# An attention and feed-forward kernel reordered by hand: woven stages, transposes by DMA, and a weight fold in fp16 halves

## Chip, cores, metric

The kernel runs on one core of a Trainium2 chip. The metric is device time in microseconds (us) of one execution. The core has five engines, each with its own queue of instructions, that meet by semaphores: TensorE (PE; its weight loads are the row PEld), VectorE (DVE), ScalarE (ACT), GpSimd (POOL) and SyncE (SP), which here only issues DMA transfers. Sixteen DMA engines carry all transfers.

Medians are over all runs of a kernel.

## The reference, cut to what matters

```
B = H = 8, S = 576 tokens, D = 64;  m = 32 landmarks, 18 tokens each
q_lm, k_lm = means of q, k over each landmark's 18 tokens
A  = softmax(q  @ k_lm.T / 8)     Bm = softmax(q_lm @ k_lm.T / 8)     C = softmax(q_lm @ k.T / 8)
Z  = Bm.T / (norm1(Bm) * norminf(Bm));   six times: Z = 2 Z - Z @ Bm @ Z
x  = A @ Z @ C @ v                        # 4608 x 512 over all batches and heads
out = ((x @ w1) * (x @ w2)) @ w3 @ w_out  # d_ff = 1024
```

Both kernels fold `w34 = w3 @ w_out` once, project `(Z C v)` through w1 and w2 per batch (`gt`), multiply by the normalised A (`up`: 64 products of 288 columns per batch), multiply the two results, and apply `w34` (`down`: 36 chunks of 128 tokens in all, 8 products of 512 columns each).

## The kernel before

The parts that the change touches. A tile scheduler may move instructions within what dependencies and buffers allow; the text order is not the issue order.

```python
CH = [(0, 128), (128, 128), (256, 128), (384, 128), (512, 64)]
    def load_attn(b):                       # 256-byte pieces: 64 floats of one head, one token
        ...
                nc.gpsimd.dma_start(out=qkn[0:sz, c, t, :]..., in_=src[b, :, s0:s0 + sz, :].rearrange("h p d -> p h d"))
    def attention(b, st):
        ...
                    nc.tensor.transpose(out=pst[:, 4 * t + r, 0:sz], in_=qkn[...], identity=ident16[...])
            ...                             # ScalarE or VectorE copies pst to qkT
                nc.vector.reduce_sum(out=lm[:, t, :, :], in_=qkT[:, t, :, :]..., axis=AX.X)
        ...                                 # qbd, B scores psB, C scores, A scores
        for it in range(6):                 # inverse chain on [residual | C v], 96 columns
            ...
                nc.vector.tensor_copy(out=nsz[:, :, 0:32], in_=pv_[:, :, 0:32])
                nc.vector.tensor_tensor(out=nsz[:, :, 32:96], in0=sz_[:, :, 32:96], in1=pv_[:, :, 32:96], op=ALU.add)
    def fold(pf):                           # fp32: TensorE transposes of w3, then products
        ...
    load(0); load_weights(); load(1)
    attention(0, sts[0]); fold(pf); attention(1, sts[1])
    for b in range(B):
        ...                                 # load(b + 2), attention(b + 1)
        project(sts[b]); up(sts[b], ab, S * (b % 2)); down(ab, t0, ...)
```

The softmax here doesn't subtract the row's maximum and nothing guards it: scores larger than these inputs give would overflow.

## Time and profile before

511.3 us (median; 510.3 to 512.5). The page's head, with the busy shares, and two rows of its picture of the span in 40 slices (tenths of busy time; tenths of full TensorE clock):

```profile
span 508.7 us, 8421 instructions
...
PE 356.7 (70%) x3584; PEld 210.3 (41%) x3584; DVE 215.1 (42%) x440; ACT 130.2 (26%) x213; POOL 80.7 (16%) x114
...
PE   0227179999765966696669476957695669476997
...
PEclk9999569999955896599659955995598669865999
```

No engine is full. The table by stretches (start:end and length; busy us and instructions for PE, PEld, DVE, ACT, POOL; granted clock; DMA share; GB/s) separates the stages:

```profile
core 0: us, PE busy (x) PEld busy (x) DVE busy (x) ACT busy (x) POOL busy (x), PEclk, DMA share, GB/s
0.00:62.00 62.00, 16.71 (x272) 10.36 (x272) 19.29 (x72) 6.69 (x11) 20.90 (x33) 0.89 1.33 200
69.00:135.00 66.00, 65.66 (x211) 33.58 (x209) 11.85 (x18) 5.45 (x9) 4.59 (x7) 0.97 0.37 63
184.00:234.00 50.00, 35.99 (x425) 21.89 (x423) 24.71 (x48) 15.72 (x26) 9.67 (x13) 0.76 0.56 71
```

Three readings. Until 62 us TensorE waits for batch 0's q and k, which come in small pieces. From 69 to 135 us the fold fills it. From 184 us every batch takes 50 us, of which TensorE is busy for 36 at a clock of 0.76. The longest chain of waits shows why: in each period one stage follows another, and a different engine holds each. These are some of its pieces in the period from 184 us (start, us, engine and line):

```profile
188.21 5.02 DVE lm L143 x2
193.25 0.43 DVE qbd L149
194.02 2.08 PE big L212 x20
...
202.60 0.90 PE small L260 x16
204.09 0.90 PE small L260 x16
...
209.95 1.06 DVE rr L297
...
217.03 8.53 PE big L342 x62
```

Line 143 is the landmark sum on VectorE, 149 the block-diagonal operand of the B scores, 212 the C scores, 260 the inverse chain (0.90 us of TensorE of every 1.49 us; most of the rest is VectorE), 297 a reciprocal, 342 the dense up products. The largest wait of TensorE from 184 to 485 us says the same (who waited for whom, us in total, times, longest):

```profile
PE small L160 <- DVE qbd L149: 37.1, 6, 6.2
```

So in every period TensorE stood 6.2 us for this operand; 5.0 us of it are the landmark sums.

### The profile page before, as it was taken

The numbers are of one execution on the slowest core, as the hardware profiler recorded it, in microseconds if no ns is written. First come the engines' busy times: TensorE is split into PE (matmuls) and PEld (weight loads), VectorE is DVE, ScalarE is ACT, GpSimd is POOL, SyncE is SP. The second block draws the span as 40 slices with busy tenths as digits, with TensorE's granted clock in tenths as the row PEclk, the third lists the DMA queues.
The fourth block names the chain that finished last, engine by engine and source line by source line (L and its number), as shares of the span: only waits on it lengthen the run. The fifth ranks groups of instructions, "written<-read, shape, count | busy, mean of one in ns | idle before, by whom it ended". The sixth has DMA issues, their size and how long they took to land.

```text
span 508.7 us, 8421 instructions
## 1 busy us (share of the span) xinstructions
PE 356.7 (70%) x3584; PEld 210.3 (41%) x3584; DVE 215.1 (42%) x440; ACT 130.2 (26%) x213; POOL 80.7 (16%) x114
## 2 busy tenths in 40 slices
PE   0227179999765966696669476957695669476997
PEld 0114054444343534363436253634353436253653
DVE  5034041111354635453545445544454454545450
ACT  0112000000220532153214321432153224322452
POOL 6231360000150025002400430034000000000000
PEclk9999569999955896599659955995598669865999
DMA  9999994120094039304920691049202000100012
GB/s 255 183 184 210 164 169 97 41 82 1 3 112 74 2 93 130 50 3 114 132 45 4 107 140 22 22 101 126 46 0 84 1 2 36 68 1 1 37 48 104
DMA packets 122037, 39.34 MB, mean 77 GB/s; under 512 B 113296, under 2 KB 113296, under 8 KB 122000
## 3 DMA queue, kind: packets, MB, share of 16 engines
q0 software_dynamic: 77120, 13.64, 33.6%
q1 hardware_dynamic: 42688, 18.88, 16.3%
q10 hardware_dynamic: 2192, 6.29, 3.4%
q8 instruction: 28, 0.46, 0.4%
q14 instruction: 9, 0.07, 0.0%
HBM read 42.99 MB, written 9.44 MB: 103 GB/s over the span
## 4 chain that ended last, share of the span: by engine, by line
PE 63%; DVE 17%; DMA 10%; ACT 5%; issue 2%; POOL 2%; ACTq 0%; POOLq 0%
PE big L342 13%; PE small L356 12%; PE small L380 11%; DVE lm L143 7%; PE small L260 6%; DMA qkn<-in_q_dram 6%; DMA qkn<-in_k_dram 5%; PE big L322 5%; PE small L227 4%; ACT qkT L137 3%; PE big L212 3%; PE small L277 2%; PE big L307 2%; DVE rr L297 2%; PE big L373 2%
## 5 line engine op out<-in xcount | busy, mean ns | idle before, releaser
L342 PE MATMUL big<-ahat,gt 128*128 128x288 f16 x512 | 71.7, 287 | 2.6 <-DVE gt L330 1.6
L106 POOL DMA_DIRECT2D qkn<-in_q_dram x40 | 35.4, 884 | 236.6 <-PE pst L132 215.3
L356 PE MATMUL small<-w_133,ab 128*128 128x512 f16 x288 | 63.5, 379 | 0.0
L342 PEld LDWEIGHTS <-gt 128*128 128x128 f16 x512 | 48.3, 97 | 28.8 <-issue 5.6
L348 DVE TENSOR_TENSOR ab<-a_sb,big 128x576 f16<-128x576 f16 x64 | 48.3, 755 | 23.1 <-ACT a_sb L347 19.6
L380 PE MATMUL small<-wof,w3t 128*128 128x512 f32 x128 | 56.7, 599 | 0.3 <-DVE w3t L377 0.3
L132 PE MATMUL pst<-ident_84,qkn 128*128 128x128 f16 (+1 forms) x320 | 24.6, 223 | 35.6 <-DMA qkn<-in_q_dram 20.8
L347 ACT CAST a_sb<-big 128x576 f16<-128x576 f32 x64 | 40.8, 638 | 31.5 <-PE big L342 31.5
L139 DVE COPY qkT<-pst 128x1024 f16<-128x1024 f16 x16 | 11.1, 692 | 81.9 <-PE pst L132 81.9
L143 DVE TENSOR_REDUCE lm<-qkT 128x128 f16<-128x2304 f16 x16 | 40.1, 2548 | 7.3 <-ACT qkT L137 7.3
L356 PEld LDWEIGHTS <-ab 128*128 128x128 f16 x288 | 28.2, 98 | 32.5
L106 POOL DMA_DIRECT2D qkn<-in_k_dram x40 | 35.2, 880 | 14.3 <-DMA wdup<-in_moe_w_dram 8.3
L132 PEld LDWEIGHTS <-qkn 128*128 128x128 f16 (+1 forms) x320 | 19.7, 100 | 42.1 <-DMA qkn<-in_q_dram 21.9
L160 PE MATMUL small<-lm,qbd 128*64 128x32 f16 x32 | 2.3, 225 | 49.4 <-DVE qbd L149 49.4
L380 PEld LDWEIGHTS small<-wof,w3t 128*128 128x128 f32 x128 | 24.1, 192 | 29.1 <-issue 28.3
L359 ACT ACTIVATE o_sb<-small 128x512 f32<-128x512 f32 x36 | 21.5, 597 | 44.7 <-PE small L356 44.7
L377 DVE COPY w3t<-big 128x512 f32<-128x512 f32 x16 | 10.7, 689 | 50.0 <-PE big L373 33.2
L283 ACT ACTIVATE zt<-small 128x256 f16<-128x256 f32 x8 | 3.1, 383 | 106.1 <-PE small L277 106.1
L137 ACT COPY qkT<-pst 128x1024 f16<-128x1024 f16 (+1 forms) x24 | 20.8, 868 | 30.0 <-PE pst L132 30.0
L322 PE MATMUL big<-wdup,zt 128*32 128x512 f16 x256 | 25.9, 575 | 0.3 <-ACT gt L328 0.3
L330 DVE TENSOR_SCALAR gt<-big 128x1024 f16<-128x1024 f32 x16 | 19.5, 1225 | 15.4 <-PE big L322 15.3
L328 ACT ACTIVATE gt<-big 128x1024 f16<-128x1024 f32 x16 | 16.3, 1023 | 35.3 <-PE big L322 35.3
(265 smaller groups left out, 344.4 us busy)
## 6 DMA issues: line engine op xcount, KB each, us to landing
out_dram<-o_sb SPq DMA_DIRECT2D x36, 256.0 KB, 2.0
vt<-in_v_dram SPq DMA_DIRECT2D x32, 256.0 KB, 4.9
w3f<-in_moe_w_dram ACTq DMA_DIRECT2D x8, 512.0 KB, 4.0
qkn<-in_q_dram POOLq DMA_DIRECT2D x32, 128.0 KB, 4.7
qkn<-in_k_dram POOLq DMA_DIRECT2D x32, 128.0 KB, 4.9
wdup<-in_moe_w_dram POOLq DMA_DIRECT2D x4, 1024.0 KB, 22.7
wof<-in_moe_w_out_dram ACTq DMA_DIRECT2D x1, 2048.0 KB, 10.8
vt<-in_v_dram SPq DMA_DIRECT2D x8, 128.0 KB, 5.0
```

The lines of the kernel that those rows point to most:

```text
L106: nc.gpsimd.dma_start(out=qkn[0:sz, c, t, :].rearrange("p (h d) -> p h d", d=D), in_=src[b, :, s0:s0 + sz, :].rearrange("h p d -> p h d"),)
L132: nc.tensor.transpose(out=pst[:, 4 * t + r, 0:sz], in_=qkn[0:sz, c, t, 128 * r:128 * r + 128], identity=ident16[0:sz, 0:sz])
L137: nc.scalar.copy(out=dst, in_=pst[:, :, 0:sz])
L143: nc.vector.reduce_sum(out=lm[:, t, :, :], in_=qkT[:, t, :, :].rearrange("p r (l g) -> p r l g", g=GRP), axis=AX.X,)
L260: nc.tensor.matmul(psI[sl, 96 * qd + (32 if last else 0):96 * qd + 96], sz_[sl, qd, 0:32], sz_[sl, qd, (32 if last else 0):96], start=True ...
L322: nc.tensor.matmul(psG[32 * h:32 * h + 32, n, :], st["zt"][:, 4 * qd + h, :], wdup[:, 4 * qd + h, w, 512 * n:512 * n + 512], start=True, s ...
L342: nc.tensor.matmul(p[:, c, 0:HS], st["g"][qd][:, w, 128 * j:128 * j + 128], st["ahat"][qd][:, c, :], start=(qd == 0), stop=(qd == 1))
L347: nc.scalar.copy(out=a_sb, in_=ps[0][:, :, 0:HS])
L348: nc.vector.tensor_tensor(out=ab[:, j, off:off + S].rearrange("p (c s) -> p c s", c=2), in0=a_sb, in1=ps[1][:, :, 0:HS], op=ALU.mult)
L356: nc.tensor.matmul(pso[:, :], ab[:, j, 128 * t:128 * t + 128], w34[:, j, :], start=(j == 0), stop=(j == 7))
L359: nc.scalar.activation(out=o_sb, in_=pso[:, :], func=AXF.Copy, scale=1.0 / (X64 * X64))
L380: nc.tensor.matmul(psW[:, :], w3t[:, c4, :], wof[:, c, :], start=(c == 0), stop=(c == 7))
```

## The change

Its intent: no scheduler, but an order written by hand, in which pieces of the attention of batch b+2 and of the inverse chain of b+1 lie between up and down products of batch b; fewer, longer load pieces; q, k and w3 transposed by DMA from on-chip memory to on-chip memory; the fold as four fp16 products of high and low halves instead of one in fp32; an inverse chain that carries only Bm-sized blocks. The diff, cut to its core (definitions of tiles and unchanged arithmetic are left out):

```diff
+    ctx.enter_context(tc.manual_schedule())
+    def load_qk(b, st):                       # 96 partitions, 6 tokens each: 1.5 KB per piece
+            nc.gpsimd.dma_start(out=n, in_=src[b].rearrange("h (p x) d -> p h (x d)", p=P))
+    def turn_qk(b, st):
+            nc.sync.dma_start_transpose(out=t.rearrange("p h j s -> p (h j) s"),
+                in_=st[name + "n"].rearrange("p h x -> p (h x)"))
-                    nc.tensor.transpose(out=pst[:, 4 * t + r, 0:sz], ...)
-            ... nc.scalar.copy / nc.vector.tensor_copy(out=dst, in_=pst[:, :, 0:sz])
+    def landmarks(b, st):
+        for name in ("k", "q"):
+            nc.vector.tensor_reduce(out=lp, in_=st[name + "T"]..., axis=AX.XY, op=ALU.add)
+            nc.vector.tensor_copy(out=lx[0:64], in_=lp[64:128])     # the two halves hold
+            nc.scalar.copy(out=lx[64:128], in_=lp[0:64])            # even and odd tokens
+        ... lmk = lp + lx;  qbd = lp + lx
...
-        for it in range(6):  # 96 columns, two VectorE operations per step
+    def istep(b, st, it):    # 64 columns, one VectorE operation
+            nc.vector.tensor_tensor(out=d4[:, :, 0:2, :], in0=s4[:, :, 0:3:2, :], in1=pv_, op=ALU.add)
...
+        def split_w3(j):
+            nc.scalar.activation(out=s[:, 0, :], in_=t, func=AXF.Copy, scale=WS)
+            nc.vector.scalar_tensor_tensor(out=s[:, 1, :], in0=t, scalar=WS, in1=s[:, 0, :], op0=ALU.mult, op1=ALU.subtract)
+            nc.sync.dma_start_transpose(out=w3t.rearrange("p a c j -> p (a c) j"), in_=s.rearrange("p a c -> p (a c)"))
+        def prod(j, c):
+            for a, bb in ((0, 0), (1, 0), (0, 1), (1, 1)):
+                nc.tensor.matmul(psw[j], w3ts[j][:, a, c, :], woh[:, c, bb, :], ...)
...
+    def spread(main, other):                  # lays `other` evenly between `main`
+    for f in fold[:16]:
+        f()
+    spread(fold[16:], front(0) + ... + back(0)[:7] + front(1) + back(0)[7:])
     for b in range(B):
+        main = []                             # 8 up units with the held down chunks of b-1 strewn in
+        ...
+            turn_qk(b + 2, sts[b + 2]); load_v(b + 2, sts[b + 2]); load_qk(b + 3, sts[b + 3])
+        ...                                   # other = front(b+2) mixed with the chain of b+1, then project(b+1)
+        spread(main, other)
+        held = [down chunks of b]
```

`front` begins with the landmarks and the B scores of its batch.

## The prediction

> **What bounds the kernel now.** The span is 508.7 us and no engine is full: the page gives TensorE 70%, VectorE 42%, ScalarE 26%. The chain of waits shows three stages. (1) Start: batch 0 waits for its q, k pieces until 62 us (113,296 of 122,037 packets are under 512 B). (2) The fp32 fold w3*w_out, 69 to 135 us: dense TensorE, 10.5 us per 24 products (437 ns each), plus transposes. (3) From 184 us, a serial period of 50.1 us per batch: 16 us of full up/down products (64 of 288 columns in 7.9 us, 32 or 40 of 512 in 6.9 or 8.65 us) and 34 us of attention and projection, where each engine waits for another: transposes and copies 4 us, landmark sums 5.0 us, 1.3 to 1.5 us per inverse step, reciprocals. There the table by stretches shows TensorE 60 to 75% busy at a granted clock of 0.5 to 0.75.
>
> **What the change does.** Emission order becomes execution order: attention of b+2 and the inverse chain of b+1 lie between up and down products of b, so latency should be paid in parallel. The TensorE transposes of q, k (24.6 us busy) and their copies (32 us on ScalarE, VectorE) go; two DMA transposes per batch replace them. Loads become 1.5 KB runs. Chain steps are 64 columns instead of 96, with one vector operation instead of two. The fold becomes 256 fp16 products (down shows 216 ns at 512 columns: 55 us against 66), which hide attention 0 and 1. Added: about 26 us of splitting on ScalarE and VectorE, GpSimd sums, a copy across partitions after the landmark sums.
>
> Transpose time is an estimate: the Trainium skill, "DMA: Bandwidth & Descriptors" (Latency and other measured facts), gives 261 GB/s for one transpose; 0.59 MB gives 2.3 us, plus its 2.0 us fixed cost: 4.3 us. No run here shows it yet.
>
> **A woven batch.** TensorE: up 7.9, down 7.8, scores 3, C*V 1.5, chain 3.5, Z, denominators, normalising 2.5, projection 2 to 3: 29 to 31 us. VectorE: up 6.0, landmarks 7.3, projection 2.4, rest 9: 25 us. TensorE bounds, but not alone: landmarks hold VectorE for 7 us in one piece, while TensorE has one down chunk and one up unit (3 us) ahead of the B scores that need them. I expect a 4 to 5 us hole per batch there: 37 us per period instead of 50 (six periods: minus 78).
>
> **Start.** Fold from about 18 to 20 us, thin until all weight pieces and first transposes are through (SyncE carries all transposes in one queue). Then 48 fold units (41 us) woven with 21 us of attention, plus stalls. First up product at about 118 us, against 169 now: minus 50. Last batch and final down: unchanged.
>
> Sum: 118 + 6x37 + 25 (batch 6: up, down, chain, projection) + 15 + 10 = 390; I shade to 383, since fuller activity should raise the granted clock.
>
> **Predicted: 383 us, 8 in 10 within 348 to 425. Faster by over 2%: 0.96; within 2%: 0.02; slower: 0.02.**
>
> **Right, if:** TensorE above 80% in the middle with clock above 0.9; period 35 to 39 us; largest TensorE wait the B scores on VectorE's landmarks; transposes landing in 4 to 6 us; fp16 fold at 216 ns each. **Wrong, if:** transposes land in over 10 us, so landmarks wait for DMA; VectorE over 85% busy; fold stretched by late weights, start beyond 130 us.
>
> **What would make it wrong.** Slow transposes (sixteen, and eight for the fold, in one queue) would push it beyond 420. If the in-order queues interlock less than I think, 345.

## The result and the profile after

The changed kernel takes 409.4 us (median of 5; fast runs 406.0 to 409.4), before 511.3 us. The ratio is 0.7975, interval 0.7943 to 0.8008. (A ratio is the mean time of one kernel's fast runs over that of the other's of the same rounds, so it is not quite the ratio of the medians.) Executions over 1.5% slower than the fastest of the same kernel are left out of the means. The measured time lies within the predicted range, 26 us above its centre. The profiled run is one of the slow ones (414.7 us), so its numbers are compared below with care.

The page's head and picture after:

```profile
span 413.0 us, 8352 instructions
...
PE 287.4 (70%) x3552; PEld 161.6 (39%) x3552; DVE 216.1 (52%) x437; ACT 128.0 (31%) x201; POOL 45.1 (11%) x72
...
PE   0007703999479847949949890898298639999995
...
PEclk9999965999959959979987996699699959999999
```

The stretches after, with the same columns:

```profile
0.00:33.70 33.70, 0.00 (x0) 0.00 (x0) 12.36 (x47) 7.51 (x7) 3.77 (x10) 1.00 1.07 228
33.70:47.70 14.00, 13.94 (x58) 6.01 (x59) 4.63 (x3) 2.60 (x3) 0.78 (x1) 1.00 1.12 257
47.70:68.30 20.60, 1.49 (x8) 0.50 (x7) 4.69 (x7) 1.40 (x3) 0.77 (x1) 0.65 1.26 158
68.30:141.00 72.70, 64.04 (x685) 29.64 (x685) 34.04 (x72) 16.73 (x25) 10.78 (x16) 0.89 0.88 147
141.00:399.00 258.00, 198.54 (x2764) 121.12 (x2761) 158.87 (x307) 96.12 (x158) 29.03 (x44) 0.89 0.45 93
```

TensorE does nothing until 33.7 us, and almost nothing again from 47.7 to 68.3 us. The loop from 141 us has TensorE busy 198.5 of 258 us, 77%, where before it was 72% of a longer period, at a clock of 0.89 instead of about 0.75. TensorE's waits over the whole run:

```profile
PE small L442 <- DMA w3t<-w3s: 60.4, 3, 33.8
PE small L157 <- DVE qbd L149: 46.7, 6, 11.7
PE small L386 <- DVE xd L239: 2.5, 2, 1.3
```

Line 442 is the fold: it waited for transposed w3 three times, 60.4 us in all. Line 157 is the B scores: six waits of 7.8 us in the mean and 11.7 at most, 46.7 us in all. Everything else is small. Between the first and the last up product the trace has six spells in which the granted clock is 0.5, and each begins within one of the six waits for the B scores. The longest wait lasts from 247.7 to 259.3 us, and the clock is 0.5 from 251.7 to 265.4 us. How long the transposes took, from issue to landing (median):

```profile
w3t<-w3s SPq DMA_TRANSPOSE x8, 12.4
kT<-nat SPq DMA_TRANSPOSE x8, 6.1
qT<-nat SPq DMA_TRANSPOSE x8, 5.4
```

The q and k transposes have medians of 6.1 and 5.4 us. Those of w3 have a median of 12.4 us, a minimum of 4.5 and a maximum of 24.9. SyncE's own queue at the start and around one landmark stage (start; us from the first instruction's start to the last one's end, gaps between them included; instructions):

```profile
8.78 24.67 SPq L432 DMA_TRANSPOSE w3t<-w3s  x2
...
34.18 8.33 SPq L78 DMA_TRANSPOSE kT<-nat  x1
...
47.70 44.93 SPq L432 DMA_TRANSPOSE w3t<-w3s  x4
```

```profile
210.25 34.62 SPq L397 DMA_DIRECT2D out_dram<-o_sb  x10
245.46 3.06 SPq L78 DMA_TRANSPOSE kT<-nat  x1
248.71 3.07 SPq L78 DMA_TRANSPOSE qT<-nat  x1
```

Of the two w3 transposes in the first line, one is issued at 8.8 us (it lands at 33.7) and the other at 21.4. In the second fence the q, k transposes are issued at 245.5 and 248.7 us, right after the ten output stores of the iteration before, the last of which waited for the last down chunk. VectorE's landmark sums then waited for both transposes (4.1 and 2.3 us), and TensorE for the sums, until 259.3 us.

### The profile page after: what moved, and what is told of

Its sections match the earlier page's. It is cut to its first block, busy times and chain, and to the rows that moved or that the text cites. A ratio compares the mean times of both kernels' runs of the same rounds, so it can differ in the third digit from the quotient of the medians.

```text
span 413.0 us, 8352 instructions
## 1 busy us (share of the span) xinstructions
PE 287.4 (70%) x3552; PEld 161.6 (39%) x3552; DVE 216.1 (52%) x437; ACT 128.0 (31%) x201; POOL 45.1 (11%) x72
## 4 chain that ended last, share of the span: by engine, by line
PE 57%; DMA 19%; DVE 14%; ACT 5%; issue 4%; SPq 0%; ACTq 0%; DVEq 0%
PE small L386 15%; DMA w3t<-w3s 14%; PE small L442 14%; PE big L373 13%; DVE lp L137 6%; DMA qT<-nat 5%; PE small L291 3%; PE big L210 3%; PE big L330 3%; PE small L232 3%; ACT a_sb L378 2%; DVE ab L379 2%; DVE gt L337 1%; PE big L248 1%; ACT gt L335 1%
## 5 line engine op out<-in xcount | busy, mean ns | idle before, releaser
L442 PE MATMUL small<-woh,w3t 128*128 128x512 f16 x256 | 67.8, 410 | 61.2 <-DMA w3t<-w3s 60.4
L373 PE MATMUL big<-ahat,gt 128*128 128x288 f16 x512 | 80.6, 304 | 0.9 <-DVE gt L337 0.5
L386 PE MATMUL small<-w,ab 128*128 128x512 f16 x288 | 69.6, 388 | 4.5 <-DVE xd L239 2.5
L442 PEld LDWEIGHTS <-w3t 128*128 128x128 f16 x256 | 24.1, 103 | 91.1 <-DMA w3t<-w3s 61.4
L373 PEld LDWEIGHTS <-gt 128*128 128x128 f16 x512 | 48.4, 103 | 22.7 <-issue 4.4
L157 PE MATMUL small<-lmk,qbd 64*32 64x32 f16 x64 | 1.9, 195 | 46.7 <-DVE qbd L149 46.7
L220 POOL TENSOR_TENSOR e<-ect 96x384 f32<-96x384 f32 x16 | 16.0, 999 | 164.5 <-ACT ect L215 82.6
L137 DVE TENSOR_REDUCE lp<-kT 128x256 f32<-128x2304 f16 x8 | 20.4, 2548 | 8.6 <-DMA kT<-nat 8.5
L137 DVE TENSOR_REDUCE lp<-qT 128x256 f32<-128x2304 f16 x8 | 20.4, 2553 | 7.5 <-DMA qT<-nat 7.4
L291 PE MATMUL small<-sz 32*32 32x64 f32 (+1 forms) x768 | 20.6, 224 | 1.5 <-DVE sz L298 1.5
L298 DVE TENSOR_TENSOR sz<-sz,small 128x128 f32<-128x128 f32 x40 | 11.4, 284 | 16.8 <-PE small L291 16.5
L429 DVE SCALAR_TENSOR_TENSOR w3s<-w3f,w3s 128x1024 f16<-128x1024 f32 x8 | 9.8, 1222 | 18.2 <-ACT w3s L428 18.2
```

Source lines behind the costliest of these rows:

```text
L137: nc.vector.tensor_reduce(out=lp, in_=st[name + "T"].rearrange("p h j (l g) -> p h l j g", g=3), axis=AX.XY, op=ALU.add)
L220: nc.gpsimd.tensor_tensor(out=e3, in0=ect[:, 0:3], in1=ect[:, 3:6], op=ALU.add)
L291: nc.tensor.matmul(psI[sl, 64 * qd:64 * qd + n], src[sl, qd, 32:64], src[sl, qd, 0:n], start=True, stop=True, tile_position=(32 * h, 32 * h))
L373: nc.tensor.matmul(p[:, c, 0:HS], st["g", qd][:, w, 128 * j:128 * j + 128], st["ahat", qd][:, c, :], start=(qd == 0), stop=(qd == 1))
L386: nc.tensor.matmul(pso[:, :], ab[:, j, 128 * t:128 * t + 128], w34[:, j, :], start=(j == 0), stop=(j == 7))
L442: nc.tensor.matmul(psw[j], w3ts[j][:, a, c, :], woh[:, c, bb, :], start=(c == 0 and a + bb == 0), stop=(c == 7 and a + bb == 2))
```

## The experiments

Twelve kernels ran. All gave correct results. Each was timed in three rounds beside the kernel before, which stayed at 509.7 to 511.4 us. To separate the start from the loop I read when the first and the last group of up products (line 373 or its counterpart) began.

| kernel | median us | ratio to before | first up, us | first to last up, us |
|---|---|---|---|---|
| changed kernel | 409.4 | 0.7975 | 141.0 | 258.5 |
| the same again | 410.8 | 0.7983 | 136.4 | 260.7 |
| early turn | 395.3 | 0.7737 | 134.5 | 242.3 |
| early turn and early sums | 400.2 | 0.7845 | 138.1 | 246.5 |
| w1, w2 load later | 418.4 | 0.8191 | 145.2 | 257.8 |
| w3 turned on TensorE | 403.0 | 0.7865 | 125.4 | 257.9 |
| no weave in the loop | 461.7 | 0.9026 | 166.5 | 276.0 |
| two operations per step | 414.1 | 0.8089 | 142.7 | 260.0 |
| chunks first | 404.9 | 0.7959 | 136.3 | 252.9 |
| copy off ScalarE | 412.3 | 0.8062 | 135.2 | 260.4 |
| chunks first, copy off ScalarE | 376.8 | 0.7353 | 136.2 | 222.2 |
| those, start mended | 357.4 | 0.6948 | 117.1 | 224.9 |
| those, fold in fp32 | 342.6 | 0.6700 | 102.3 | 231.7 |

(The "no weave" loop emits attention before its first up unit, so its two columns are not comparable with the others. The last two columns are of the profiled run alone. The profiles of the changed kernel, "the same again", "two operations" and "fold in fp32" fell in slow runs.) Kernels with the start of the changed kernel show the first up product at 134.5 to 138.1 us in fast profiles, and at 136.4 and 141.0 us in the two slow ones, so differences of a few us in that column mean nothing.

**The changed kernel again.** Unaltered, beside other variants.

> The changed kernel once more, unaltered, to have it on the same chip and in the same rounds as the variants beside it, and a profile in the fast state. Expected 405 to 410 us; first up product at 138 to 142 us, TensorE's wait for the B scores' operand 44 to 48 us.

As expected in its times (median 410.8 us; fast runs 406.2 and 409.3) and its waits (47.6 us for the B scores); the first up product, at 136.4 us, came a little before the stated range.

### What made the loop wait

**Early turn.** Theory A blames SyncE's queue order, theory B the VectorE work itself.

```diff
+        if b + 3 < B:
+            fr.insert(8, lambda n=b + 3: bring(n))   # turn_qk, load_v, next load_qk: mid iteration
-        if b + 2 < B: turn_qk(b + 2, ...) ...        # was: start of the next iteration
```

> Only the place of the q, k DMA transposes in SyncE's queue changes: those of batch b+3 are issued in the middle of iteration b instead of at the start of iteration b+1, so they no longer stand behind that iteration's last output stores. Theory A (queue order: the hole before the B scores is partly the late transposes): VectorE's waits for the kT and qT DMA (16 us in all) vanish from the middle, TensorE's wait of 46.7 us on qbd (six waits, mean 7.8, longest 11.7) falls to about 30 us (mean 5), and the time falls by 10 to 16 us. Theory B (the hole is VectorE's own 7 to 8 us of landmark work): the wait stays above 42 us and the time moves by under 5 us.

Measured 395.3 us. VectorE's waits for kT and qT fell from 15.9 us to 0.5, and TensorE's wait became:

```profile
PE small L157 <- DVE qbd L149: 32.7, 6, 7.0
```

Six waits of 5.5 us, four of them of 5.2. Theory A is confirmed for 14 us of waiting (12 to 13 us of time by the ratios). What remains is a wait for VectorE's landmark work, which itself hardly waits for a transpose any more; the prediction had put it at 4 to 5 us.

**Early turn and early sums.** The sums also move to the end of the iteration before, in three pieces.

```diff
+            other.insert(k3 - 7, lambda: lm_sum(n3, s3, "k"))
+            other.insert(k3 - 3, lambda: lm_sum(n3, s3, "q"))
+            other.append(lambda: lm_join(n3, s3))
+        if b > 0 and fr:
+            fr.pop(0)                                # landmarks no longer at the head of front
```

> As the early turn, and the landmark sums of batch b+3 are also made at the end of iteration b, in three pieces laid between other work, instead of in one piece in front of the B scores. Theory A+B (both late transposes and the 7 us piece): TensorE's wait on qbd falls under 8 us and the time falls by 25 to 40 us against the changed kernel. Rival (VectorE is nearly full, the sums only move the hole): the wait goes to other VectorE results (gt, ab, psum slots) and the time falls by under 15 us.

Measured 400.2 us, 5 us slower than the early turn. The wait for the B scores fell to 10.7 us, and new ones came:

```profile
PE big L336 <- ACT a_sb L384: 13.8, 6, 2.9
PE small L163 <- DVE qbd L150: 10.7, 5, 7.0
PE small L392 <- DVE xd L245: 7.7, 2, 3.9
```

The rival holds: the hole moved, here to the projection (line 336), which waits for PSUM that ScalarE has not yet emptied.

**Chunks first.** Instead of moving the sums, give TensorE work under them: the down chunks need no VectorE, only a copy by ScalarE.

```diff
+        main = ups
+        if fr:
+            other.pop(0)()          # landmarks(b + 2)
+        for f in held:              # then all 4 or 5 down chunks
+            f()
         spread(main, other)
```

> Only the order in an iteration changes: landmarks of b+2, then all held down chunks (4 or 5, 7 to 8.7 us of TensorE that need only ScalarE to drain), then up units woven with the rest. Theory: the hole before the B scores is TensorE running out of work that does not need VectorE; the chunks fill it and the output stores leave SyncE's queue early. Then TensorE's wait on qbd falls from 46.7 to under 10 us and the time falls by 25 to 35 us, to 372 to 384. Rival (as the early sums showed: VectorE's 25 us then collect behind the up units instead): the time falls by under 16 us, no better than the early turn alone.

Measured 404.9 us: five of the six waits for the B scores are gone (the one left, 5.7 us, is in the first iteration), and the time has hardly moved. TensorE's waits and ScalarE's queue in one landmark stage:

```profile
PE small L386 <- ACT o_sb L389: 22.7, 5, 4.5
...
PE small L157 <- DVE qbd L149: 5.7, 1, 5.7
```

```profile
206.88 0.40 ACT L142 COPY lx<-lp 64x256 f32<-64x256 f32 x1 [4.35 <-DVE lp L137]
209.79 0.40 ACT L142 COPY lx<-lp 64x256 f32<-64x256 f32 x1 [2.51 <-DVE lp L137]
210.22 1.08 ACT L389 ACTIVATE o_sb<-small 128x512 f32<-128x512 f32 x2
```

ScalarE's next instruction after the projection was `lx` (line 142), the copy of the landmark sums' other half. It waited 4.35 us and then 2.51 us for VectorE's sums. The chunks' output copies (line 389) were behind it, so two finished chunks kept both small PSUM buffers (TensorE's result memory) until ScalarE began to empty them at 210.2 us. TensorE stood meanwhile, 22.7 us in five such waits. The Trainium skill, "TensorE: Matmul & The Clock Gate" (the table at its head), calls the queues of ScalarE, VectorE and GpSimd "strict FIFO"; this trace agrees.

**Chunks first, and the copy off ScalarE.** One line more.

```diff
-            nc.scalar.copy(out=lx[64:128], in_=lp[0:64])
+            nc.vector.tensor_copy(out=lx[64:128], in_=lp[0:64])
```

> As the chunks first, with one line more: the copy of the landmark sums' lower half into the upper partitions is made by VectorE, not ScalarE. Theory: in the chunks-first run ScalarE stood in its queue at this copy, which waits for VectorE's 2.5 us sums, so the chunks' output copies behind it came late and TensorE ran out of PSUM (22.7 us on o_sb in five waits). Then those waits fall under 4 us and the time falls by 15 to 24 us against chunks first, to 381 to 390. Rival (TensorE's freed time is only given back behind VectorE, which gets 0.6 us more per batch): under 8 us.

Measured 376.8 us, 28 us less than with the order alone in the medians and 31 by the ratios, more than expected.

```profile
PE small L291 <- DVE sz L298: 9.6, 7, 1.5
PE small L157 <- DVE qbd L149: 7.6, 4, 6.3
```

The loop of chunks first, and of this kernel, with the columns of the stretches above:

```profile
136.00:389.00 253.00, 199.69 (x2770) 119.20 (x2763) 158.55 (x309) 95.67 (x158) 29.09 (x44) 0.94 0.48 96
136.20:358.40 222.20, 190.33 (x2767) 117.20 (x2764) 162.06 (x320) 91.48 (x147) 29.05 (x44) 0.98 0.55 110
```

The wait on `o_sb` is gone from the table, the one on qbd is 7.6 us, and the loop has shrunk to 222.2 us, with TensorE busy 190 us of it, 86%. The gain over chunks first is larger than the 22.7 us of waits because TensorE's busy time fell as well, by 9 us, at a granted clock of 0.98 instead of 0.94.

**The copy alone.** The fourth corner: the one-line edit just shown, made in the changed kernel without the new order.

> The changed kernel with only the copy of the landmark halves moved from ScalarE to VectorE, the order left as it is: the fourth corner beside the changed kernel (about 409), chunks first (405) and both (377). If the two only work together (in the given order TensorE stands at the B scores anyway, and what ScalarE holds back has nobody waiting): within 6 us of the changed kernel, wait on qbd still above 40 us. If the copy on ScalarE was the fault by itself: faster by 15 us or more.

Measured 412.3 us, wait on qbd 50.8 us. So of two edits that alone change next to nothing (ratios 0.7959 and 0.8062, against 0.7975 and 0.7983 of the changed kernel), both together are worth 32 us (0.7983 less 0.7353, times 510). In the order as given TensorE stood at the B scores in any case, and no large wait on ScalarE shows; with the order mended, the copy was the next thing in the way. (That the same copy spoiled the early sums, too, is likely, since line 336 waited for ScalarE, but no run took it away there.)

**No weave.** How much is the weaving worth at all?

```diff
-        spread(main, other)
+        for f in other: f()
+        for f in main: f()
```

> In each iteration of the loop all attention pieces of later batches are emitted first, then the held down chunks and up units; nothing else differs (the start is still woven, chain and attention of two batches are still mixed). If the gain of the loop comes from laying latency under up and down products: period 42 to 46 us instead of 36, time 440 to 465 us. Rival (the gain comes from the shorter work itself: no TensorE transposes, no copies, shorter chain, and weaving adds little since the engines block each other in order): time under 425 us.

Measured 461.7 us. The ratio says that the loop's weave gives about 53 us of the 103 us gained (0.9026 against 0.7983, times 510). The rest, by subtraction, is the start and the shorter work; no run separates these two. Without the weave TensorE's clock in the loop is back at 0.75, and its waits for the sums grow from 47.6 to 64.0 us, those for the chain (line 298) from 1.5 to 9.6. In the middle the first up products of two batches lie 44 to 48 us apart, a little above the stated 42 to 46.

**Two operations per step.** The chain's one VectorE operation becomes two again, still on 64 columns.

```diff
-            nc.vector.tensor_tensor(out=d4[:, :, 0:2, :], in0=s4[:, :, 0:3:2, :], in1=pv_, op=ALU.add)
+            for i in range(2):
+                nc.vector.tensor_tensor(out=d4[:, :, i, :], in0=s4[:, :, 2 * i, :], in1=pv_[:, :, i, :], op=ALU.add)
```

> Each inverse step's addition is cut into two VectorE operations, as the kernel before had it: 40 more operations of about 0.2 us, 8 us of VectorE in all. If the chain's latency is hidden under other work: the time rises by under 4 us. If the chain still bounds: it rises by 8 us or more.

Measured 414.1 us, between the two marks: the means of fast runs differ by 5.4 us. The loop in the profile, 260.0 us, is not longer than that of the same kernel again (260.7), and the difference lies before the first up product (142.7 against 136.4 us), where two runs of one kernel differed by 4.6. Both profiles are of slow runs. So the chain's latency appears to be hidden in the loop; the total is inconclusive.

### What made the start late

**The w1, w2 load later.**

```diff
-    load_weights()
     turn_qk(0, sts[0])
     load_qk(1, sts[1])
+    load_weights()
```

> The 4.2 MB load of w1, w2 is issued after batch 1's q, k loads instead of before them. Theory C (the first two weight transposes, issued at 8.8 us and landed at 33.7, are slow because they share the 16 DMA engines with 7 MB of loads): they land by about 20 us, fold starts there, and the time falls by 5 to 14 us, some given back where the load now meets the next transposes. Rival D (transposes are slow by themselves): first fold product stays at 30 us or later and the time does not fall.

The first fold product came at 21.8 us instead of 33.8, so the first transposes had been slowed by the loads beside them (theory C), and D falls. But the time rose by 9 us in the medians, 11 by the ratios. The first two lines are of the changed kernel, the others of this one:

```profile
33.76 15.42 PE L442 MATMUL small<-woh,w3t 128*128 128x512 f16 x64 [33.76 <-DMA w3t<-w3s]
68.29 5.30 PE L442 MATMUL small<-woh,w3t 128*128 128x512 f16 x12 [19.11 <-DMA w3t<-w3s]
...
21.76 16.38 PE L442 MATMUL small<-woh,w3t 128*128 128x512 f16 x64 [21.76 <-DMA w3t<-w3s]
61.77 5.30 PE L442 MATMUL small<-woh,w3t 128*128 128x512 f16 x12 [23.64 <-DMA w3t<-w3s]
...
82.72 1.89 PE L442 MATMUL small<-woh,w3t 128*128 128x512 f16 x4 [9.21 <-DMA w3t<-w3s]
```

The load now met the next transposes, and the fold's second wait became 23.6 us, with a third of 9.2. The collision was only moved. My expectation had the sign of the total wrong.

**w3 turned on TensorE.** The same halves, transposed through PSUM (16 transposes of 128x128 per block).

```diff
-            nc.sync.dma_start_transpose(out=w3t..., in_=s...)
+            for a in range(2):
+                for c in range(8):
+                    nc.tensor.transpose(out=pst[:, a, c, :], in_=s[:, a, 128 * c:128 * c + 128], identity=ident16[:, :])
+            nc.scalar.copy(out=w3t[:, 0], in_=pst[:, 0])
+            nc.vector.tensor_copy(out=w3t[:, 1], in_=pst[:, 1])
```

> The w3 halves are transposed on TensorE (16 of 128x128 per block, through PSUM, half copied by ScalarE and half by VectorE) instead of by DMA. If the 60.4 us that TensorE waited for w3t are the cost of the start, the fold starts at about 12 us, its middle gaps go, the first up product comes at 110 to 118 us instead of 141, and the time falls by 22 to 32 us. Rival: the fold is then held by the weight loads themselves (last w_out piece landed at 22 us) or by q, k of batch 0, and under 12 us come back.

Measured 403.0 us, about 6 us less. The first up product came at 125.4 us, 9 to 13 us earlier than in the fast profiles with the start as it was; the loop was unchanged. (This profile is of the kernel's fastest run, 398.5 us.) The rival was nearer: the fold's first products came at 27.8 us, not 12. TensorE turned the first half at 11.4 us, but the copies of the result stood in ScalarE's queue behind the splitting of later pieces, the last of which waited for its load of w_out until 25.7 us. TensorE's two longest waits (first line: B scores; second: turning of w3):

```profile
PE small L159 <- DVE qbd L151: 58.2, 8, 11.9
PE pst L441 <- ACT w3s L430: 19.1, 2, 11.4
```

**Start mended.** The mended loop, w3 turned on TensorE, w1, w2 loaded later (now harmless), and seven fold units in a row while the landmarks of batches 0 and 1 are made.

```diff
+    gap = [lambda: None] * 7
+    pro = (f0[:1] + gap + f0[1:] + ... + f1[:1] + gap + f1[1:] + back(0)[7:])
```

> The former, plus the start mended: w3 halves turned on TensorE, the w1, w2 load behind batch 1's q, k (now no weight transposes are left for it to meet), and seven fold units in a row while landmarks of batches 0 and 1 are made. First up product at 105 to 115 us against 136 to 141; time lower than the former by 22 to 35 us, 350 to 365. Rival (start bound by load bandwidth): first up product still after 122 us.

Measured 357.4 us; first up product at 117.1 us. 19 us less than the mended loop alone, a little under the expected 22 to 35 (21 by the ratios). The three changes of the start were made together, so their shares are not known.

**The fold in fp32.** As the kernel before computed it, in the mended kernel.

```diff
-        (split_wo, split_w3; four fp16 products per unit)
+            nc.tensor.transpose(out=pst[:, c, :], in_=s[:, 128 * c:128 * c + 128], identity=ident[:, :])   # fp32
+            nc.tensor.matmul(psw[j], w3ts[j][:, c, :], wof[:, c, :], start=(c == 0), stop=(c == 7))
```

> The former, with the fold as the kernel before computed it, in fp32 (64 products, which that trace shows as 128 records of 437 ns: 56 us against 55 for 256 fp16 products), so the splitting of w3 and w_out, 26 us of ScalarE and VectorE, goes, and only 64 transposes remain, of about 0.15 us. If the fp16 halves only repay what they cost: within 6 us of the former either way. If they were worth having: slower by over 8 us.

Measured 342.6 us, another 15 us less in the medians and 13 by the ratios, which none of the stated outcomes had. The first fold product comes at 17.9 us instead of 27.8, the last at 100.8 instead of 115.8:

```profile
L453 PE MATMUL small<-woh,w3t x256: 379/379/634, 27.8 to 115.8; 128*128 128x512 f16 x128
```

```profile
L435 PE MATMUL small<-wof,w3t x128: 592/592/1061, 17.9 to 100.8; 128*128 128x512 f32 x128
```

The span of products is about as long (83 against 88 us): in both kernels a whole block of w3 takes 7.0 to 7.1 us of TensorE where it runs dense. What goes is the splitting between load and transpose, and half of the transposes and copies. The order of the first loads changed as well (w3 before w_out), so the 10 us by which the fold begins earlier are not shown to be due to the splitting alone. Against the changed kernel this version is about 65 us faster by the ratios, and it beats both kernels.

## Why the prediction was right or wrong

- **Direction and range: right.** 409.4 us in 348 to 425. The sum of its terms was 390, shaded to 383.
- **The term that was mis-sized is the start.** "First up product at about 118 us" measured 141.0 and 136.4 us (134.5 to 138.1 in fast profiles of kernels with the same start). The step that failed in it is "Fold from about 18 to 20 us": it began at 33.8 us, and stood again until 68.3. The prediction had the single queue of transposes right, but took their time as 4.3 us each. For q and k in the loop, most of them 5.0 us and none over 8.3, that was nearly right; for w3, beside 160 to 260 GB/s of transfers up to 68 us, the median is 12.4 us and the worst 24.9. Its own test ("start beyond 130 us") caught this. The rest of the sum fits the profiled run: 141.0 us, six periods of 37.1 and 49.6 for the end make its span of 413 us, where the prediction had 118, 37 and 50.
- **"37 us per period": right in size, for partly other reasons.** From the first up product of batch 0 (141.0 us) to that of batch 6 (363.4 us) the six periods take 37.1 us each. TensorE's hole at the B scores was there, the largest wait of the loop as foreseen, but 7.8 us and not 4 to 5. Some 2.3 us of the hole are transposes behind output stores in SyncE's queue (early turn: 14 us over six waits). TensorE's own work was smaller than the 29 to 31 us of the sum: 27 us of busy time per period (163.4 us over the six). A hole taken 3 us too small and work taken 2 to 4 us too large offset each other, which is luck.
- **"TensorE above 80% in the middle with clock above 0.9": missed,** 77% and 0.89 over the loop, 73% and 0.88 over the six periods. The clock did rise, from 0.75, but the shade from 390 to 383 for it led away from the result. The Trainium skill, "TensorE: Matmul & The Clock Gate" (Part 1), says that the clock is halved after about an idle window of 3.4 us. This trace agrees: each of the loop's six holes, 4.9 to 11.7 us long, brought one spell of half clock, and with the holes gone the mean is 0.98.
- **"The fold becomes 256 fp16 products ... 55 us against 66": the rate was right, the worth was not.** Dense pieces ran 44 products in 9.66 us, 220 ns each, which makes 56 us for 256; the 64 products in fp32 (128 records) took 56.7 us in the kernel before. The 66 us include 9 us of transposes that the change needs as well, by DMA, and the first of the splitting lay on the path to the first product. The fp32 fold was 13 to 15 us faster in the mended kernel; in the changed kernel itself it was not tried.
- **Weaving pays latency in parallel: right.** Without it 461.7 us.
- **Not foreseen:** that ScalarE's copy in the landmark stage would stop everything behind it. Moving it gained nothing in the kernel as changed, and 28 to 31 us as soon as the order was mended.

Open: why executions of the changed kernel spread from 406 to 415 us, and why transposes beside loads take up to five times as long as the fastest; the later load of w1 and w2 shows that the loads do it, not by what mechanism.

## What to carry to other kernels

In a hand-woven order an instruction that waits holds up what stands behind it in its queue, as ScalarE's copy and SyncE's output stores did here: for each engine, and for SyncE's transfers, ask what stands in front of an instruction that others wait for, and put work that needs only free engines under the longest piece on a busy one. When mending one wait brings nothing, read the waits again before undoing it: here two edits were worth next to nothing alone and 32 us together. Transposes by DMA came cheap here where few other transfers ran and nothing stood before them in the queue; at a start full of loads TensorE did them sooner.

## What the Trainium skill lacked or had wrong

- "DMA: Bandwidth & Descriptors" (Latency and other measured facts) gives 261 GB/s for one transpose. That rate plus the page's fixed cost of about 2 us makes 4.0 us, an estimate, for the 512 KB of a w3 block, and the fastest one landed in 4.5 us, so it roughly holds. It lacks what happens beside loads: the same size took up to 24.9 us.
- "Advanced Engine Details and Errata" (X-Bar Transpose (TRN2)) says that transposes are as fast as regular DMAs. Beside other loads that did not hold here: of a load of w_out and a transpose of w3, both of 512 KB and issued at 8.8 us, the load landed in 9.1 us and the transpose in 24.9. (Over the whole run the medians for 512 KB are 4.4 and 8.0 us for loads of w3 and w_out, and 12.4 for the transposes; the fastest transpose, 4.5 us, was like a load.)
- No page that I read has how much the time varies for which the issuing instruction of a transpose holds its queue: for w3 blocks of one size it was 1.3 to 12.1 us of SyncE each, for q and k in the loop 2.9 to 3.7 us.
